# The first batch of an attention and feed-forward kernel, reordered as a pipeline: exponentials in a row, padding behind the first copies, second batch's scores and loads earlier, tail scores in one tile

## Chip, cores, metric

One core of a Trainium2 chip. The metric is the device time of one execution in microseconds (us), lower is better. Most executions of one kernel agree within a few tenths of a per cent, but some spread more (six of the changed kernel in e5: 431.95 to 436.08); all runs told here are of the fast state. A profile is one execution recorded by the hardware profiler; its span is the time from the first to the last instruction, some 1.8 us shorter than the time of the same execution.

## The reference

Attention with a relative position bias, then a bilinear feed-forward layer.

```python
B, H, S, D = 8, 8, 576, 64           # q, k, v: (8, 8, 576, 64), float32
scores = (q @ k^T) / 8 + bias[bucket(|i - j|)]          # bias per head
attn   = softmax(scores)
x      = (attn @ v), heads side by side                 # (4608, 512)
out    = ((x @ w_a) * (x @ w_b)) @ w_out                # d_ff = 1536
```

## The kernel before

The program is ordered by hand: each engine executes its instructions in the order in which the program gives them. Two heads are a "pair" `p`; there are 32 pairs, 4 for each of the 8 batches. A sequence of 576 is 512 main positions and 64 tail positions. The bias is applied after the exponential, as a multiplication by a stored band of exponentiated bias (`W_sb`, `Wt_sb`).

The first batch (pairs 0 to 3) runs by itself, in halves of 256 queries, because nothing else can run yet. From pair 4 on there is a "stage" `s` for each pair: scores and exponentials of pair `s`, outputs of pair `s-1`, and between them "units" of the feed-forward layer. A unit is four matmuls of 128x512 (0.86 to 0.88 us of TensorE), or of 128x256 for the first chunk's split part (0.44 us). `quotas` says how many units a stage gets; from stage 9 on it is 9.

```python
def padding():                       # constants: zeros and ones around the loaded values
    for i in range(2):
        nc.vector.memset(vt[i][0:64, :, 1, :], 0.0)
        ...                          # 12 memsets in all
# ... warm-up matmuls, bias table ...
nc.vector.tensor_copy(out=tab_sb[0:H, c0:c0 + NR], in_=tps[0:H, 0:NR])
padding()                            # VectorE: before any copy of q or k
# ... loads of q, k, v, weights, in the order of the diff below ...

def t_qk(p):                         # transpose q, k of a pair on TensorE, copy out of PSUM
    t_q(p, ACT if p == 0 else None)  # None: VectorE
    t_k(p, None, ps_ff)
def scores0(p, h):                   # scores of half h, then two exponentials on ScalarE
    qk_half(p, h); ex_half(p, h, 0); ex_half(p, h, 1)
def scale0(p, h):                    # two multiplications by the bias band on VectorE
    mul_half(p, h, 0); mul_half(p, h, 1)
    if h == 1: mul_tail(p)

def t_x(p, jqs=range(5), eng=None):  # transpose the outputs of a pair for the feed-forward layer
    if 4 <= p < NP - 1:
        ...                          # by two DMA transposes, issued by SyncE
        return
    ...                              # pairs 0 to 3 and 31: on TensorE, copied by eng

for c in range(NCH):                 # 9 chunks of 512 tokens
    if c == 0:
        parts = [(range(0, 6), 0, 256), (range(0, 6), 256, 256), (range(6, NDF), 0, 512)]
    else:
        parts = [(range(NDF), 0, 512)]
    ...                              # units of x@w_a, x@w_b, then 12 units of @w_out
```

`warm_up(n)` puts `n` dummy matmuls on TensorE. `av(p, jqs)` computes attention outputs and normalizes them on VectorE.

The softmax here doesn't subtract the row's maximum and nothing guards it: scores larger than these inputs give would overflow.

## Time and profile before

| | before |
|---|---|
| time, median of 3 | 436.48 us (435.53 to 437.32) |
| span of the profile | 434.5 us |
| TensorE busy | 410.5 us (94%) |
| first scores of the second batch (stage 4) | 41.37 us |
| stage 5, stage 8, stage 9 begin | 52.36, 81.84, 91.31 us |

The page of the kernel before shows busy tenths in 40 slices of the span (10.9 us each), and the clock granted to TensorE in tenths:

```profile
PE   6768799999999999999999999999999999999995
DVE  5577667656664666466745664566546651321320
ACT  3767667566665676566666665676566633223321
PEclk8999999999999999999999999999999999999999
```

TensorE (PE) is full from the sixth slice. Only the first 55 us hold idle time that could be won; after that every microsecond is one of matmuls. VectorE (DVE) and ScalarE (ACT) are not full anywhere, so in the first slices no engine is the limit: they wait for one another.

The order in time of ScalarE before, at the start (start, duration, engine, line, operation, output and input; in brackets the idle time before it and what ended it):

```profile
5.30 0.60 ACT L277 ACTIVATE QT_105<-trb 128x512 bf16<-128x512 bf16 x1 [2.12 <-PE trb L287]
8.54 1.02 ACT L378 ACTIVATE ath_0_0_273<-qkh_0_0_263 128x1024 bf16<-128x1024 f32 x1 [2.65 <-PE qkh_0_0_263 L372]
...
13.31 1.02 ACT L378 ACTIVATE ath_0_0_352<-qkh_0_0_342 128x1024 bf16<-128x1024 f32 x1
...
15.13 1.03 ACT L378 ACTIVATE ath_0_0_368<-qkh_0_0_358 128x1024 bf16<-128x1024 f32 x1
...
17.92 1.02 ACT L395 ACTIVATE att_113<-qkt_384 128x1024 bf16<-128x1024 f32 x1 [0.84 <-PE qkt_384 L393]
```

The `ath` rows are the exponentials of pairs 0, 2 and 3; the last is that of the tail keys, which ends the first half of the batch. A row takes 1.02 us but the next can start 0.92 us later. From 17.92 us, 23.45 us pass until stage 4, with 8 more exponentials and 4 tails in them (about 11 us of work at the pitch of these rows).

VectorE before, the end of the padding and the first copy:

```profile
4.56 0.28 DVE L182 MEMSET vt_103<- 64x260 bf16 x1
...
7.15 0.11 DVE L188 MEMSET XG_121<- 64x64 uint32 x1
7.29 0.42 DVE L279 COPY KT_109<-trk_234 128x512 bf16<-128x512 bf16 x1
```

The transposed k of pair 0 was ready at 5.6 us (its transposes start at 5.20 and take 0.41) and waited for the padding.

The stretches view for stages 4 to 8 of the kernel before: length, busy time of each engine, in parentheses instructions, then granted clock, DMA share, GB/s:

```profile
core 0: us, PE busy (x) PEld busy (x) DVE busy (x) ACT busy (x) POOL busy (x), PEclk, DMA share, GB/s
41.37:52.36 10.99, 9.32 (x109) 6.65 (x110) 6.52 (x16) 7.23 (x15) 2.97 (x4) 1.00 1.28 204
52.36:63.08 10.72, 9.90 (x108) 5.74 (x109) 7.17 (x19) 7.32 (x13) 9.79 (x14) 1.00 1.54 128
63.08:72.74 9.66, 9.51 (x99) 4.92 (x101) 7.13 (x17) 7.13 (x11) 8.18 (x13) 1.00 1.90 174
72.74:81.84 9.10, 8.93 (x86) 4.54 (x86) 6.18 (x16) 5.74 (x9) 5.33 (x8) 1.00 1.75 116
81.84:91.31 9.47, 8.57 (x83) 4.50 (x85) 4.83 (x13) 6.05 (x9) 4.49 (x7) 1.00 1.03 171
```

Stages 4 and 5 leave TensorE some room (9.32 of 10.99, 9.90 of 10.72), stages 6 and 7 almost none.

### The profile page before, as it was taken

Reading aid. Unit: us, or ns where it says so; the run is one execution under the profiler, and the core shown is the slowest. Engines: PE = TensorE matmul, PEld = TensorE weight load, DVE = VectorE, ACT = ScalarE, POOL = GpSimd, SP = SyncE. Lnnn points to the kernel's source line nnn. Section 1 sums busy time; section 2 is a strip of 40 time slices with the busy share of each in tenths; the row PEclk is TensorE's granted clock in tenths of the full one; section 3 lists DMA queues with packets and bytes.
Section 4 is the critical chain, followed back from the end, with each engine's and each line's share of the span. In section 5 each row is a group of like instructions: output and inputs, shape, how many; then the busy total and the mean of one; then the engine's idle time right before and its main releaser. Section 6 shows DMA issues by size and latency. Waiting matters only on the chain.

```text
span 434.5 us, 8785 instructions
## 1 busy us (share of the span) xinstructions
PE 410.5 (94%) x3426; PEld 210.0 (48%) x3477; DVE 238.9 (55%) x582; ACT 250.2 (58%) x362; POOL 130.0 (30%) x187
## 2 busy tenths in 40 slices
PE   6768799999999999999999999999999999999995
PEld 3446555445445544445455545454555454444442
DVE  5577667656664666466745664566546651321320
ACT  3767667566665676566666665676566633223321
POOL 9654398295009600780059004300000000000000
PEclk8999999999999999999999999999999999999999
DMA  9999999999339943998279907960420011002004
GB/s 124 203 209 189 202 119 175 142 142 157 55 63 142 157 78 63 116 157 103 48 104 161 128 16 112 140 87 16 88 84 6 15 39 74 0 9 89 0 2 97
DMA packets 139596, 42.46 MB, mean 98 GB/s; under 512 B 115962, under 2 KB 134938, under 8 KB 139554
## 3 DMA queue, kind: packets, MB, share of 16 engines
q0 software_dynamic: 81264, 18.89, 50.4%
q1 hardware_dynamic: 52850, 13.54, 20.6%
q10 hardware_dynamic: 5440, 9.47, 6.7%
q8 instruction: 27, 0.44, 0.4%
q14 instruction: 15, 0.12, 0.1%
HBM read 39.18 MB, written 9.45 MB: 112 GB/s over the span
## 4 chain that ended last, share of the span: by engine, by line
PE 86%; DVE 6%; ACT 4%; issue 2%; DMA 0%; ACTq 0%; DVEq 0%
DVE g_140 L520 1%; PE po_0_1422 L527 1%; PE po_0_2701 L527 1%; PE po_0_4581 L527 1%; PE po_0_3963 L527 1%; PE po_0_3332 L527 1%; PE po_0_2070 L527 1%; PE po_3_2846 L527 1%; PE po_3_4108 L527 1%; PE po_3_2215 L527 1%; PE po_3_3477 L527 1%; PE po_3_4726 L527 1%; PE po_3_5742 L527 1%; PE po_2_4698 L527 1%; PE po_2_3449 L527 1%
## 5 line engine op out<-in xcount | busy, mean ns | idle before, releaser
L158 POOL DMA_DIRECT2D vt_104<-in_v_dram x8 | 4.9, 619 | 62.4 <-PE av_3_2771 L467 27.6
L517 PEld LDWEIGHTS <-wb_126 128*128 128x128 bf16 x152 | 14.5, 97 | 18.6 <-issue 4.2
L507 PEld LDWEIGHTS <-wa_122 128*128 128x128 bf16 x160 | 15.1, 98 | 17.2 <-issue 1.8
L517 PEld LDWEIGHTS <-wb_125 128*128 128x128 bf16 x160 | 14.0, 97 | 18.1 <-issue 8.0
L507 PEld LDWEIGHTS <-wa_124 128*128 128x128 bf16 x144 | 13.3, 98 | 18.3 <-issue 3.4
L158 POOL DMA_DIRECT2D vt_103<-in_v_dram x8 | 5.0, 650 | 53.8 <-PE av_3_3402 L467 27.1
L507 PEld LDWEIGHTS <-wa_123 128*128 128x128 bf16 x152 | 13.2, 98 | 15.3 <-issue 3.6
L129 POOL DMA_DIRECT2D qn_93<-in_q_dram x24 | 18.4, 815 | 7.2 <-DMA wo<-in_moe_w_out_dram 5.9
L517 PEld LDWEIGHTS <-wb_127 128*128 128x128 bf16 x144 | 12.4, 97 | 16.6 <-issue 6.3
L138 POOL DMA_DIRECT2D kn_95<-in_k_dram x24 | 18.1, 800 | 3.7 <-PE av_2_847 L467 1.9
L129 POOL DMA_DIRECT2D qn_94<-in_q_dram x24 | 18.1, 802 | 1.1 <-DMA vt_103<-in_v_dram 0.6
L138 POOL DMA_DIRECT2D kn_96<-in_k_dram x24 | 18.1, 790 | 0.3 <-PE pb_9_0_1283 L517 0.3
L527 PEld LDWEIGHTS <-g_137 128*128 128x128 bf16 x36 | 3.5, 97 | 8.7 <-issue 6.8
L520 DVE TENSOR_TENSOR g_133<-pb_0_0_5542,ha_0_0_5540 128x512 bf16<-128x512 f32 x1 | 0.7, 692 | 11.4 <-PE pb_0_0_5542 L517 11.4
L205 PE MATMUL warm<-zero_sb 128*128 128x512 bf16 x13 | 5.6, 535 | 1.4 <-DVE zero_sb L197 1.2
L120 POOL DMA_DIRECT2D vn_97<-in_v_dram x8 | 6.3, 784 | 1.5 <-DVE rc_0_1185 L476 0.7
L120 POOL DMA_DIRECT2D vn_98<-in_v_dram x8 | 6.3, 784 | 1.1 <-DVE g_135 L520 0.8
L349 PEld LDWEIGHTS <-KB_116 64*128 64x128 bf16 x96 | 2.9, 94 | 7.5 <-issue 6.4
L527 PEld LDWEIGHTS <-g_133 128*128 128x128 bf16 x36 | 3.5, 98 | 4.6 <-issue 0.8
L527 PEld LDWEIGHTS <-g_139 128*128 128x128 bf16 x36 | 3.5, 98 | 4.3
L527 PEld LDWEIGHTS <-g_140 128*128 128x128 bf16 x36 | 3.5, 98 | 4.2
L527 PEld LDWEIGHTS <-g_135 128*128 128x128 bf16 x36 | 3.5, 98 | 4.3
(2939 smaller groups left out, 1524.7 us busy)
## 6 DMA issues: line engine op xcount, KB each, us to landing
vn_97<-in_v_dram POOLq DMA_DIRECT2D x8, 256.0 KB, 5.9
vn_98<-in_v_dram POOLq DMA_DIRECT2D x8, 256.0 KB, 6.6
wo<-in_moe_w_out_dram POOLq DMA_DIRECT2D x1, 1536.0 KB, 16.4
kn_95<-in_k_dram POOLq DMA_DIRECT2D x24, 64.0 KB, 5.4
qn_93<-in_q_dram POOLq DMA_DIRECT2D x24, 64.0 KB, 4.8
kn_96<-in_k_dram POOLq DMA_DIRECT2D x24, 64.0 KB, 4.6
qn_94<-in_q_dram POOLq DMA_DIRECT2D x24, 64.0 KB, 4.6
qn_93<-in_q_dram POOLq DMA_DIRECT2D x4, 128.0 KB, 4.2
```

The lines of the kernel that those rows point to most:

```text
L120: nc.gpsimd.dma_start(out=dst[:, 256 * h0:256 * h1].rearrange("p (h x) -> p h x", x=256), in_=src[b, h0:h1, 0:SM, :].rearrange("h (p t) d ...
L129: nc.gpsimd.dma_start(out=by_tile(qn[b % 2])[:, h0 // 4, t, :, :], in_=q[b, h0:h1, 128 * t:128 * t + 128, :].transpose([1, 0, 2]))
L138: nc.gpsimd.dma_start(out=by_tile(kn[b % 2])[:, h0 // 4, t, :, :], in_=k[b, h0:h1, t:SM:NM, :].transpose([1, 0, 2]))
L158: nc.gpsimd.dma_start(out=vt[b % 2][64 * hh:64 * hh + 64, :, hh, 0:Dh], in_=v[b, hh:H:2, SM:S, :].transpose([1, 0, 2]))
L205: nc.tensor.matmul(out=warm[:, :], lhsT=zero_sb[:, 0:128], rhs=zero_sb[:, :], start=True, stop=True)
L349: nc.tensor.matmul(out=ps[:, hh, :], lhsT=kT[r, t, :], rhs=qT[r, :, :], start=True, stop=True)
L507: nc.tensor.matmul(out=pa[:, 0:n], lhsT=wa_sb[df // 4][:, mc, 128 * (df % 4):128 * (df % 4) + 128], rhs=xn_sb[mc][:, 512 * c + lo:512 * c ...
L517: nc.tensor.matmul(out=pb[:, 0:n], lhsT=wb_sb[df // 4][:, mc, 128 * (df % 4):128 * (df % 4) + 128], rhs=xn_sb[mc][:, 512 * c + lo:512 * c ...
L520: nc.vector.tensor_tensor(out=g_sb[df][:, lo:lo + n], in0=pb[:, 0:n], in1=ff["ha"][:, 0:n], op=MULT)
L527: nc.tensor.matmul(out=po[:, :], lhsT=g_sb[df][:, 128 * tt:128 * tt + 128], rhs=wo_sb[:, df, :], start=(df == 0), stop=(df == NDF - 1))
```

## The change

The intent: let the exponentials of the first batch follow one another without gaps, so that the second batch's scores start earlier. The padding moves from in front of the first copies to behind the copies of pair 1; seven of the eight copies of attention outputs (`t_x`) go from ScalarE to VectorE; the tail scores of a first-batch pair share one PSUM tile and take one exponential and two multiplications instead of two and three (the later pairs keep two exponentials, but also take two multiplications instead of three); the loads of the second batch's q and k move ahead of weights. The feed-forward units are cut anew: the first chunk is split for four weight tiles instead of six (44 units instead of 48), only 4 of them stand before stage 4 instead of 8, and stages 6 and 7 get 7 instead of 6.

```diff
-    padding()                                   # (was in front of the first copies)
-            parts = [(range(0, 6), 0, 256), (range(0, 6), 256, 256), (range(6, NDF), 0, 512)]
+            parts = [(range(0, 4), 0, 256), (range(0, 4), 256, 256), (range(4, NDF), 0, 512)]
...                                              # tail: scores of tail x tail into the main tail tile
+        pt = ps[:, 1, n:n + ST] if n < SM else tr_half().bitcast(FP32)[:, 0:ST]
...
+    t_qk(0); warm_up(1); scores0(0, 0); t_qk(1)
+    padding()
+    load_rest()             # loads: q, k of batch 1 before parts 1 and 2 of the weights, w_out last
+    warm_up(1); scores0(1, 0); t_qk(2); scale0(0, 0)
+    warm_up(2); scores0(2, 0); t_qk(3); load_w_rest(); scale0(1, 0)
+    warm_up(2); scores0(3, 0); t_tails0(); scale0(2, 0); tail_keys0(); v_in(0, 0, 4)
+    sc(0, 0); sc(0, 1); av(0, h0); scale0(3, 0); tail0(0); av(1, h0, ps_ff, "ffn"); sc(1, 0)
...                          # sc: one tile of scores and its exponential; 4 units in all
-    quotas = {4: 12, 5: 8, 6: 6, 7: 6, 8: 6}
+    quotas = {4: 12, 5: 8, 6: 7, 7: 7, 8: 6}
...                          # stage 4: t_x(2), t_x(3) on VectorE, av(3) later
```

(The new lines of the order are put on fewer lines here; three dots mark cuts.)

More of the change, by code (lines that the diff above doesn't have):

```diff
@@ L99 @@
     KT = [wpool.tile([128, NM, 128], BF16, name=f"KT{i}") for i in range(4)]
-    att0 = wpool.tile([128, 4, 256], BF16, name="att0")
+    att = [wpool.tile([128, 1024 + 128], BF16, name=f"att{i}") for i in range(2)]
+    atk = wpool.tile([128, 4, 256], BF16, name="atk")
     QB = [wpool.tile([128, 2, NM, 2, 128], BF16, name=f"QB{i}") for i in range(2)]
@@ L188, in padding @@
             nc.vector.memset(XG[i][64:128, 4, :, :], 0.0)
+            nc.vector.memset(att[i][:, 512 + SM // 2 + ST:], 0.0)
     nc.sync.dma_start(out=bt_sb[0:NB, :], in_=bias_table)
@@ L243 @@
         load_k(0, h, h + 2)
-    load_tails(0)
-    load_v(0, 0, 4)
-    load_vt(0)
-    load_v(0, 4, 8)
-    load_w_in(0)
-    load_q(1, 0, 2)
-    load_k(1, 0, 2)
-    load_tails(1)
-    load_w_in(1)
-    load_q(1, 2, 4)
-    load_k(1, 2, 4)
-    load_v(1, 0, 4)
-    load_vt(1)
-    load_w_in(2)
-    load_q(1, 4, 6)
-    load_k(1, 4, 6)
-    load_w_out()
-    load_q(1, 6, 8)
-    load_k(1, 6, 8)
-    load_v(1, 4, 8)
     st = [dict() for _ in range(NP)]
@@ L362, in mul, with qk_half @@
                                 in1=w[:, :, S - 1 + t:S - 1 + t - SM:-1], op=MULT)
-    def qk_half(p, h):
+    def qk_half(p, h, us=(0, 1)):
         qT, kT, _ = operands(p)
-        for u in range(2):
+        for u in us:
             ps = ps_sc.tile([128, 2, 512], FP32, tag="sc", name=f"qkh{p}_{h}_{u}")
@@ L394, in tail_keys0 @@
                              rhs=qT[:, 0:2, :], start=True, stop=True)
-        nc.scalar.activation(out=att0[:, :, :].rearrange("p (a b) c -> p a (b c)", a=2),
+        nc.scalar.activation(out=atk[:, :, :].rearrange("p (a b) c -> p a (b c)", a=2),
                              in_=ps[:, :, :], func=ACTF.Exp, scale=scale)
@@ L405, in qk_tail @@
                 lhsT=kT[:, t, :], rhs=z[:, 0, :], start=True, stop=True)
-        q0 = 2 if p < 4 else 0
-        nc.tensor.matmul(out=ps[:, 1, 0:SM - 128 * q0], lhsT=z[:, 1, :], rhs=qT[:, q0:, :],
+        n = main_tail(p)
+        nc.tensor.matmul(out=ps[:, 1, 0:n], lhsT=z[:, 1, :], rhs=qT[:, (SM - n) // 128:, :],
                          start=True, stop=True)
-        pt = tr_half().bitcast(FP32)[:, 0:ST]
+        pt = ps[:, 1, n:n + ST] if n < SM else tr_half().bitcast(FP32)[:, 0:ST]
         for hh in range(2):
@@ L413, in qk_tail, with main_tail @@
         st[p]["ps"] = (ps, pt)
+    def main_tail(p):
+        return SM // 2 if p < 4 else SM
     def ex_tail(p):
-        hp = p % 4
         ps, pt = st[p]["ps"]
-        at = wrk.tile([128, ST + 1024], BF16, tag="att", name=f"att{p}")
-        nc.scalar.activation(out=at[:, 0:ST], in_=pt, func=ACTF.Exp, scale=scale)
-        n = 768 if p < 4 else 1024
-        nc.scalar.activation(out=at[:, ST:ST + n],
-                             in_=ps[:, :, :].rearrange("p a x -> p (a x)")[:, 0:n],
+        n = main_tail(p)
+        at = att[p % 2]
+        m = 512 + n
+        if n < SM:
+            m += ST
+        else:
+            nc.scalar.activation(out=at[:, m:m + ST], in_=pt, func=ACTF.Exp, scale=scale)
+        nc.scalar.activation(out=at[:, 0:m], in_=ps[:, :, :].rearrange("p a x -> p (a x)")[:, 0:m],
                              func=ACTF.Exp, scale=scale)
@@ L426, in mul_tail @@
     def mul_tail(p):
-        hp = p % 4
-        at, w, wt = st[p]["att"], W_sb[hp], Wt_sb[:, hp, :]
-        nc.vector.tensor_tensor(out=at[:, 0:ST], in0=at[:, 0:ST], in1=wt[:, ST - 1::-1], op=MULT)
-        x = at[:, ST:ST + 512].rearrange("p (h t c) -> p h t c", h=2, t=NM)
+        at, w, wt = st[p]["att"], W_sb[p % 4], Wt_sb[:, p % 4, :]
+        x = at[:, 0:512].rearrange("p (h t c) -> p h t c", h=2, t=NM)
         rev = w[:, :, ST - 1::-1]
@@ L434, in mul_tail @@
         nc.vector.tensor_tensor(out=x, in0=x, in1=e, op=MULT)
-        o = ST + 512 + (128 if p < 4 else 384)
-        nc.vector.tensor_tensor(out=at[:, o:o + 128], in0=at[:, o:o + 128],
-                                in1=wt[:, 191:63:-1], op=MULT)
+        o = 512 + main_tail(p) - 128
+        nc.vector.tensor_tensor(out=at[:, o:o + 192], in0=at[:, o:o + 192], in1=wt[:, 191::-1], op=MULT)
     def weights(p, t, hh, jq):
         if jq == 4:
-            o = ST + 256 * hh + ST * t
+            o = 256 * hh + ST * t
             return st[p]["att"][:, o:o + 128]
@@ L449, in weights_tail @@
         if jq == 4:
-            return st[p]["att"][:, 0:128]
+            o = 512 + main_tail(p)
+            return st[p]["att"][:, o:o + 128]
         if p < 4 and jq < 2:
-            return att0[:, p, 128 * jq:128 * jq + 128]
-        o = ST + 512 + 128 * (jq if p >= 4 else jq - 2)
+            return atk[:, p, 128 * jq:128 * jq + 128]
+        o = 512 + 128 * (jq if p >= 4 else jq - 2)
         return st[p]["att"][:, o:o + 128]
@@ L592, in tail0, with load_rest @@
         ex_tail(p)
+    def load_rest():
+        load_tails(0)
+        load_v(0, 0, 4)
+        load_vt(0)
+        load_v(0, 4, 8)
+        load_w_in(0)
+        load_q(1, 0, 2)
+        load_k(1, 0, 2)
+        load_tails(1)
+        load_q(1, 2, 4)
+        load_k(1, 2, 4)
+        load_w_in(1)
+        load_v(1, 0, 4)
+        load_vt(1)
+        load_q(1, 4, 6)
+        load_k(1, 4, 6)
+        load_w_in(2)
+        load_q(1, 6, 8)
+        load_k(1, 6, 8)
+        load_v(1, 4, 8)
+        load_w_out()
@@ L594 @@
     t_qk(0)
+    warm_up(1)
+    scores0(0, 0)
     t_qk(1)
-    scores0(0, 0)
+    padding()
+    load_rest()
+    warm_up(1)
+    scores0(1, 0)
+    t_qk(2)
+    scale0(0, 0)
     warm_up(2)
-    t_qk(2)
-    scores0(1, 0)
-    warm_up(2)
+    scores0(2, 0)
     t_qk(3)
     load_w_rest()
-    scale0(0, 0)
-    scores0(2, 0)
+    scale0(1, 0)
     warm_up(2)
     scores0(3, 0)
-    scale0(1, 0)
     t_tails0()
+    scale0(2, 0)
     tail_keys0()
     v_in(0, 0, 4)
-    scores0(0, 1)
-    warm_up(2)
@@ L613, with sc @@
-    av(0, (0, 1))
-    scale0(2, 0)
-    av(1, (0, 1), ps_ff, "ffn")
-    t_x(0, (0, 1), ACT)
-    v_in(0, 4, 8)
+    h0 = (0, 1)
+    h1 = (2, 3, 4)
+    def sc(p, u):
+        qk_half(p, 1, (u,))
+        ex_half(p, 1, u)
+    sc(0, 0)
+    sc(0, 1)
+    av(0, h0)
     scale0(3, 0)
     tail0(0)
-    av(2, (0, 1))
-    t_x(1, (0, 1), ACT)
-    scores0(1, 1)
-    av(3, (0, 1), ps_ff, "ffn")
-    t_x(2, (0, 1), ACT)
-    scale0(0, 1)
-    t_x(3, (0, 1), ACT)
-    tail0(1)
-    av(0, (2, 3, 4))
@@ L629 @@
-    scale0(1, 1)
+    av(1, h0, ps_ff, "ffn")
+    sc(1, 0)
+    v_in(0, 4, 8)
+    mul_half(0, 1, 0)
+    mul_half(0, 1, 1)
+    t_x(0, h0)
+    sc(1, 1)
+    av(2, h0)
+    mul_tail(0)
+    tail0(1)
+    t_x(1, h0)
+    av(3, h0, ps_ff, "ffn")
+    sc(2, 0)
+    mul_half(1, 1, 0)
+    av(0, h1)
+    mul_half(1, 1, 1)
+    t_x(2, h0)
+    sc(2, 1)
+    mul_tail(1)
+    tail0(2)
+    t_x(3, h0)
     t_tails(1)
-    qk_half(2, 1)
-    ex_half(2, 1, 0)
+    mul_half(2, 1, 0)
+    sc(3, 0)
+    t_x(0, h1, ACT)
@@ L634 @@
+    av(1, h1)
     put_units(1)
-    ex_half(2, 1, 1)
-    av(1, (2, 3, 4))
-    t_x(0, (2, 3, 4), ACT)
+    mul_half(2, 1, 1)
+    sc(3, 1)
+    t_q(4)
+    mul_tail(2)
     put_units(1)
-    tail0(2)
-    put_units(1)
-    scale0(2, 1)
-    t_x(1, (2, 3, 4), ACT)
-    qk_half(3, 1)
-    ex_half(3, 1, 0)
-    put_units(1)
-    ex_half(3, 1, 1)
-    av(2, (2, 3, 4))
-    put_units(1)
-    t_q(4)
     tail0(3)
-    put_units(1)
     t_k(4, ACT)
-    scale0(3, 1)
-    t_x(2, (2, 3, 4), ACT)
+    mul_half(3, 1, 0)
@@ L655 @@
+    av(2, h1)
+    t_x(1, h1)
     put_units(2)
+    mul_half(3, 1, 1)
+    mul_tail(3)
     load_half(2, 0)
     load_half(2, 1)
-    quotas = {4: 12, 5: 8, 6: 6, 7: 6, 8: 6}
+    quotas = {4: 12, 5: 8, 6: 7, 7: 7, 8: 6}
     for s in range(4, NP + 1):
@@ L667 @@
         if s == 4:
-            steps += [U, A(2, 3, 4), lambda: ex(s, 1), U, lambda: mul(s, 0), lambda: t_q(s + 1), U,
-                      lambda: mul(s, 1), lambda: t_x(s - 1, (2, 3, 4), ACT),
-                      lambda: (qk(s, 2), ex(s, 2)), U,
-                      lambda: ex(s, 3), lambda: t_k(s + 1, ACT), U,
+            steps += [U, lambda: ex(s, 1), lambda: t_x(2, h1), lambda: mul(s, 0), U, lambda: av(3, h1),
+                      lambda: t_q(s + 1), U, lambda: mul(s, 1), lambda: (qk(s, 2), ex(s, 2)),
+                      lambda: t_x(3, h1), U, lambda: ex(s, 3), lambda: t_k(s + 1, ACT), U,
                       lambda: mul(s, 2), U, lambda: mul(s, 3), U,
```

## The prediction

> **What bounds it now.** The stretches view gives TensorE 99% busy from 100 us on (19.64 of 20.00 us, 59.27 of 60.00). A row of twelve 512-wide matmuls takes 2.59 us, 216 ns each, which is the warm start-to-start that the Trainium skill gives ("TensorE: Matmul & The Clock Gate", "Wait — 56ns, not 53.3ns?"). So after the start the kernel is fixed TensorE work, and only the first ~60 us can give anything. There the chain of waits hops between all three engines. The first batch runs from 4.7 us to 41.37 us, where the first scores of the second batch (stage 4) issue. Its TensorE work, summed from the rows' pitches, is about 20 us of those 36.7. ScalarE has about 24.5 us of work there, in pieces with gaps of 1 to 2 us (an attention output copy waits for TensorE, the next exponential waits behind it). Stage 4 (41.37 to 52.5) and stage 5 (52.5 to 63.15) hold about 8.5 and 9.0 us of TensorE work, so some 2.6 and 1.7 us of slack. Stages 6 and 7 are nearly full.
>
> **What changes, costed.**
> - Padding (2.7 us of memsets, 4.56 to 7.29) stood before the first KT copy. Now that copy runs at about 5.7, and the first exponential starts near 6.5 instead of 8.54. But the padding then delays the copies of pair 2 to about 11.2, so ScalarE idles about 2 us there; the exponentials of tail keys start near 17 (17.92). Only about 1 us of the first 2 survives.
> - From there exponentials follow every 0.92 us. Seven of eight attention copies leave ScalarE in the first batch (0.38 or 0.50 us each) for VectorE.
> - Tail exponential in one: the two starts are 0.12 us apart, so 0.1 us saved for each of 4 tails; the merged multiplication saves about 0.1 us each.
> - VectorE becomes the limit of the first batch: about 27.5 us of work up to stage 4, nearly without gaps from 18 us. Walking the new order with the measured pitches (0.60 us a multiplication, 0.55 or 0.95 an output) puts the first stage-4 scores at 34 to 35.5.
> - Only 4 feed-forward units instead of 8 come before stage 4: 4 x 0.44 = 1.8 us given back. Stage 5 gets 8 full units instead of 4 half and 4 full: the same work, put into its slack. Units per chunk fall from 48 to 44 with the same matmul columns.
> - Loads: the same bytes, second-batch q and k ahead of weights, output weights last. I expect no new wait: weights part 1 land near 36 (needed about 45), part 2 near 46 (needed about 55). The rest of the bias bands land at 20.7 to 27.4 now and about 0.6 later afterwards, while needed from 21.8: one VectorE wait of up to 1 us.
>
> **Sum.** 6.5 us at stage 4, minus 1.8, plus 1 to 1.5 in stage 4, plus 1 in stages 5 to 7: about 7 us. All of it stays, since TensorE is full afterwards.
>
> Predicted 429.5 us, range 427.0 to 432.8; faster by over 2% 0.17, within 2% 0.82, slower 0.01.
>
> **What would show it.** First exponential near 6.5; first second-batch scores near 35 (41.37 now); stage 5 near 45.5 (52.5); stage 8 near 75 (81.84) with 38 of 44 units done; beyond 110 us the same 45.3 us per batch; VectorE over 90% busy from 20 to 36.
>
> **What would make it wrong.** Bias bands landing later than 28 (stalls VectorE, up to 2 us lost); the DMA order making the second batch's values or third batch's loads late; chunk boundaries now fall at the first unit of a stage, so a late transposed output of the last pair would stall TensorE once per batch; or in-order TensorE blocked behind VectorE more often than I walked through.

## The result

The change is 0.9% faster. Ratios here and below are the mean time of one kernel's fast runs over that of the kernel before in the same rounds, so they are not quite the ratio of the medians.

| | before | after |
|---|---|---|
| time, median of 4 | 436.31 us (435.53 to 437.32) | 432.19 us (432.11 to 432.51) |
| ratio, 95% interval | | 0.9906 (0.9884 to 0.9927) |
| span of the profile | 434.5 us | 430.5 us |
| first exponential | 8.54 us | 7.08 us |
| exponential of the tail keys | 17.92 us | 19.16 us |
| stage 4 begins | 41.37 us | 37.26 us |
| stage 5, 8, 9 begin | 52.36, 81.84, 91.31 | 48.21, 80.17, 89.33 |

The same lines of the page after:

```profile
PE   8689899999999999999999999999999999999995
DVE  5789667566654665466646664666546642321320
ACT  4676676676656666676566665676566642323221
PEclk9789999999999999999999999999999999999999
```

TensorE is busier in the first slices (in part because its matmuls took longer there, see the clock below), VectorE is 80% full or more in the third and fourth (21 to 43 us). The clock row now dips in the second and third slices, where before it dipped a little in the first.

ScalarE after, the exponentials that answer to those shown of before:

```profile
7.08 1.02 ACT L359 ACTIVATE ath_0_0_214<-qkh_0_0_204 128x1024 bf16<-128x1024 f32 x1 [1.11 <-PE qkh_0_0_204 L353]
...
13.67 1.02 ACT L359 ACTIVATE ath_0_0_330<-qkh_0_0_320 128x1024 bf16<-128x1024 f32 x1 [1.85 <-PE qkh_0_0_320 L353]
...
16.60 1.02 ACT L359 ACTIVATE ath_0_0_374<-qkh_0_0_364 128x1024 bf16<-128x1024 f32 x1 [0.99 <-PE qkh_0_0_364 L353]
...
19.16 1.02 ACT L376 ACTIVATE atk<-qkt_390 128x1024 bf16<-128x1024 f32 x1 [0.63 <-PE qkt_390 L374]
```

The first exponential is 1.5 us earlier than before, that of pair 2 already 0.4 us later, that of pair 3 1.5 us later, and the tail keys' 1.2 us later. The opening was to gain 1 us and lost 1.2.

VectorE after: the second copy, the padding, and the copy of pair 2's k behind it:

```profile
8.76 0.41 DVE L260 COPY KT_110<-trk_227 128x512 bf16<-128x512 bf16 x1
9.17 0.28 DVE L183 MEMSET vt_103<- 64x260 bf16 x1
...
12.12 0.19 DVE L190 MEMSET att_114<- 128x160 uint32 x1
12.23 0.63 DVE L260 COPY QT_107<-trb 128x512 bf16<-128x512 bf16 x1
12.77 0.41 DVE L260 COPY KT_111<-trk_306 128x512 bf16<-128x512 bf16 x1
```

The padding takes 3.06 us (9.17 to 12.23) and stands exactly between two pairs. TensorE has pair 2's transposes done by 10.8 us and can only wait. In the stretches view after, one microsecond at a time:

```profile
11.00:12.00 1.00, 0.35 (x2) 0.00 (x0) 0.57 (x6) 0.82 (x1) 0.00 (x0) 1.00 1.46 219
12.00:13.00 1.00, 0.00 (x0) 0.00 (x0) 0.92 (x4) 0.00 (x0) 0.94 (x2) 1.00 1.52 235
13.00:14.00 1.00, 0.76 (x10) 0.34 (x10) 1.00 (x3) 0.33 (x1) 1.00 (x2) 0.75 1.57 200
14.00:15.00 1.00, 1.00 (x18) 0.83 (x18) 0.72 (x2) 1.00 (x2) 1.00 (x3) 0.50 1.62 175
```

The third number from the right is the granted clock. After the idle stretch it falls to half, from 13.5 to 16.9 us, and again from 20.3 to 23.7 us. The Trainium skill ("TensorE: Matmul & The Clock Gate", "What's actually happening") says that the array runs at half clock unless it has been busy in a free-running window of about 3.4 us; the two dips here last 3.4 us each, which agrees.

The view writes a clock of 1.00 for all the time before 13 us, but TensorE's rows show half speed there too. Eight transposes of one shape take 0.64 us up to about 10 us, and 0.41 us from then on:

```profile
7.40 0.64 PE L268 MATMUL trb<-ident,qn_93 128*64 128x128 bf16 x8
...
10.17 0.41 PE L268 MATMUL trb<-ident,qn_93 128*64 128x128 bf16 x8
```

In the profile before they take 0.41 us already at 5.20 us, and a half-clock stretch follows from 8.4 to 11.9 us. So the two openings were not seen at the same clock, and the 1.2 us lost at the tail keys are not the padding's alone. The section on e4 puts the profiles side by side.

The stages after, in the same view as before:

```profile
core 0: us, PE busy (x) PEld busy (x) DVE busy (x) ACT busy (x) POOL busy (x), PEclk, DMA share, GB/s
37.26:48.21 10.95, 9.71 (x112) 6.98 (x113) 8.34 (x25) 6.79 (x13) 5.36 (x7) 1.00 1.44 190
48.21:60.03 11.82, 11.43 (x107) 5.74 (x109) 7.91 (x18) 7.95 (x13) 5.38 (x8) 1.00 1.63 181
60.03:70.55 10.52, 10.38 (x103) 5.32 (x104) 7.75 (x17) 7.29 (x11) 9.85 (x15) 1.00 1.90 161
70.55:80.17 9.62, 9.42 (x89) 4.98 (x90) 5.79 (x14) 6.12 (x9) 8.29 (x13) 1.00 1.80 149
80.17:89.33 9.16, 8.84 (x84) 4.50 (x86) 4.66 (x12) 6.21 (x9) 4.95 (x8) 1.00 1.66 172
```

Stage 4 is as long as before (10.95 against 10.99). Stages 5 to 7 took 31.96 us against 29.48, 2.48 more, for work worth four full units more (about 3.5 us), so they gained 1.0.

### The profile page after: what moved, and what is told of

Read it like the earlier page. It is cut to its first block, busy times and chain, and to the rows that moved or that the text cites. A ratio compares the mean times of both kernels' runs of the same rounds, so it can differ in the third digit from the quotient of the medians.

```text
span 430.5 us, 8709 instructions
## 1 busy us (share of the span) xinstructions
PE 412.0 (96%) x3406; PEld 210.3 (49%) x3459; DVE 238.0 (55%) x560; ACT 248.1 (58%) x346; POOL 130.0 (30%) x187
## 3 DMA queue, kind: packets, MB, share of 16 engines
q10 hardware_dynamic: 5440, 9.47, 7.1%
## 4 chain that ended last, share of the span: by engine, by line
PE 88%; DVE 7%; issue 2%; ACT 1%; DVEq 0%; ACTq 0%
PE warm L207 1%; DVE g_143 L505 1%; PE trb L268 1%; DVE att_113 L419 1%; PE po_2_4609 L512 1%; PE po_2_3999 L512 1%; PE po_2_3376 L512 1%; PE po_2_2753 L512 1%; PE po_2_2130 L512 1%; PE po_1_2670 L512 1%; PE po_1_3916 L512 1%; PE po_3_5650 L512 1%; PE po_0_5379 L512 1%; PE po_0_5084 L512 1%; PE po_0_3878 L512 1%
## 5 line engine op out<-in xcount | busy, mean ns | idle before, releaser
L492 PEld LDWEIGHTS <-wa_124 128*128 128x128 bf16 x160 | 14.7, 98 | 17.8 <-issue 3.9
L502 PEld LDWEIGHTS <-wb_128 128*128 128x128 bf16 x144 | 13.3, 97 | 20.3 <-issue 7.1
L159 POOL DMA_DIRECT2D vt_104<-in_v_dram x8 | 4.9, 626 | 58.9 <-PE av_3_2722 L452 27.7
L159 POOL DMA_DIRECT2D vt_103<-in_v_dram x8 | 5.1, 645 | 55.5 <-PE av_3_3345 L452 27.4
L139 POOL DMA_DIRECT2D kn_96<-in_k_dram x24 | 18.1, 795 | 0.2 <-PE pb_11_0_1307 L502 0.2
L419 DVE TENSOR_TENSOR att_113<-att_113,W_88 128x512 bf16<-128x512 bf16 x8 | 3.4, 426 | 14.2 <-ACT att_113 L409 14.2
L408 ACT ACTIVATE att_114<-trb 128x64 bf16<-128x64 f32 x14 | 3.1, 224 | 10.8 <-PE trb L392 10.8
L408 ACT ACTIVATE att_113<-trb 128x64 bf16<-128x64 f32 x14 | 3.1, 224 | 10.7 <-PE trb L392 10.7
L419 DVE TENSOR_TENSOR att_114<-att_114,W_91 128x512 bf16<-128x512 bf16 x8 | 3.4, 427 | 7.6 <-ACT att_114 L409 7.6
L121 POOL DMA_DIRECT2D vn_97<-in_v_dram x8 | 6.6, 828 | 0.0
```

Of the source, the lines that this page charges most:

```text
L121: nc.gpsimd.dma_start(out=dst[:, 256 * h0:256 * h1].rearrange("p (h x) -> p h x", x=256), in_=src[b, h0:h1, 0:SM, :].rearrange("h (p t) d ...
L139: nc.gpsimd.dma_start(out=by_tile(kn[b % 2])[:, h0 // 4, t, :, :], in_=k[b, h0:h1, t:SM:NM, :].transpose([1, 0, 2]))
L159: nc.gpsimd.dma_start(out=vt[b % 2][64 * hh:64 * hh + 64, :, hh, 0:Dh], in_=v[b, hh:H:2, SM:S, :].transpose([1, 0, 2]))
L408: nc.scalar.activation(out=at[:, m:m + ST], in_=pt, func=ACTF.Exp, scale=scale)
L419: nc.vector.tensor_tensor(out=x, in0=x, in1=e, op=MULT)
L492: nc.tensor.matmul(out=pa[:, 0:n], lhsT=wa_sb[df // 4][:, mc, 128 * (df % 4):128 * (df % 4) + 128], rhs=xn_sb[mc][:, 512 * c + lo:512 * c ...
```

## The experiments

Two questions: why stage 4 began at 37.26 and not near 35, and what happened to the gains afterwards. The theories for the opening are the padding (its 3.06 us stand on the chain between pair 1 and pair 2) and the clock (TensorE ran at half speed in two stretches). Twelve kernels ran, five rounds each beside the kernel before; all were correct, e1 to e4 on one chip and e5 to e12 on another. Where a run's expectation names a time of the changed kernel, it is the 432.2 us of the first measurement; on the other chip the same kernel measured 433.0, and the kernel before 437.7 in the same rounds, so across chips the ratios are to be compared and not the medians.

| run | stage 4 | stage 5 | stage 8 | stage 9 | third score tile of stage 9 | span | median us | ratio (95%) |
|---|---|---|---|---|---|---|---|---|
| before | 41.37 | 52.36 | 81.84 | 91.31 | 96.90 | 434.5 | 436.31 | 1 |
| after | 37.26 | 48.21 | 80.17 | 89.33 | 94.35 | 430.5 | 432.19 | 0.9906 (0.9884, 0.9927) |
| e1 padding in gaps | 34.84 | 45.80 | 77.68 | 86.85 | 93.02 | 429.2 | 432.25 | 0.9895 (0.9865, 0.9926) |
| e2 padding first | 36.06 | 47.01 | 78.89 | 88.06 | 93.09 | 429.3 | 431.57 | 0.9875 (0.9847, 0.9902) |
| e3 more warm-ups | 35.75 | 46.71 | 79.01 | 88.18 | 94.03 | 430.2 | 431.82 | 0.9891 (0.9856, 0.9927) |
| e4 e1 and e3 | 35.54 | 46.49 | 78.37 | 87.53 | 93.53 | 429.6 | 431.38 | 0.9869 (0.9842, 0.9897) |
| e5 after again | 37.87 | 48.82 | 80.92 | 90.08 | 96.72 | 432.9 | 433.01 | 0.9903 (0.9865, 0.9941) |
| e6 e1, stage 8 shorter | 35.13 | 46.09 | 77.97 | 85.42 | 91.66 | 429.2 | 431.32 | 0.9860 (0.9832, 0.9889) |
| e7 old units | 37.21 | 47.53 | 76.60 | 85.55 | 90.58 | 430.9 | 431.52 | 0.9866 (0.9838, 0.9894) |
| e8 old load order | 37.75 | 48.70 | 80.58 | 89.75 | 94.79 | 430.9 | 432.59 | 0.9883 (0.9853, 0.9913) |
| e9 e1 and e7 | 34.92 | 45.24 | 73.94 | 83.15 | 88.17 | 428.6 | 430.73 | 0.9848 (0.9817, 0.9878) |
| e10 e1, pair 7 on TensorE | 36.92 | 47.87 | 79.81 | 89.86 | 94.89 | 430.4 | 430.71 | 0.9848 (0.9819, 0.9877) |
| e11 e9, stages 5 to 7 filled | 35.50 | 45.82 | 76.82 | 86.29 | 91.88 | 429.4 | 431.78 | 0.9873 (0.9843, 0.9902) |
| e12 one copy earlier in stage 4 | 36.09 | 47.21 | 79.15 | 88.32 | 94.98 | 431.1 | 433.07 | 0.9901 (0.9870, 0.9931) |

Times at stages are of one profile each (us from the start of the span). They compare only between kernels with the same units: e6, e7, e9 and e11 have done other numbers of units by stage 8. The intervals are 0.5 to 0.8% wide, so most differences of 1 to 2 us between two of these kernels are not settled by times alone; the profile has to carry them. The gains asked about here are hardly larger than the scatter.

### e1: the padding taken apart

```diff
     nc.vector.tensor_copy(out=tab_sb[0:H, c0:c0 + NR], in_=tps[0:H, 0:NR])
+    pad_vt(0)                     # 4 memsets, VectorE idle here for 1.41 us
...
     scores0(0, 0)
+    pad_rest()                    # 6 small memsets
     t_qk(1)
-    padding()
...
     v_in(0, 0, 4)
+    pad_vt(1)                     # 4 memsets; the loads behind it are issued after it
```

> The changed kernel with its padding taken apart: first value-tail tile's memsets before the first KT copy, the small memsets after it, the second tile's after the first value copy, where VectorE idled (gaps of 1.41, 1.77 and 1.83 us). Padding theory (the 3.06 us of memsets between the pair-1 and pair-2 copies held the opening): exponential of pair 2 starts at 11 to 11.5 instead of 13.67, tail-key exponential at 17 or earlier instead of 19.16, second batch's first scores 1.5 to 2.2 us earlier than 37.26, time 1.5 to 2.2 us under the changed kernel's 432.2, so near 430.3. Clock theory (TensorE at half its clock at 13 to 16.5 and 20 to 23.6 us held it): under 0.7 us.

Measured: exponentials of pairs 1 and 2 run together from 9.42 us, so pair 2's first at about 11.3; the tail keys' at 16.86; stage 4 at 34.84, 2.4 us earlier than after; the clock was full from about 7 us on and did not fall again. The opening behaves as the padding theory says. The time did not follow: 432.25 us where 430.3 was expected. The 2.4 us of lead are still there at stage 9 (86.85 against 89.33) and shrink to 1.3 at its third scores (93.02 against 94.35). TensorE's rows of e1 in between:

```profile
86.85 0.82 PE L332 MATMUL qk<-QB,KB 64*128 64x512 bf16 x4
87.60 0.82 PE L494 MATMUL pa<-xn,wa 128*128 128x512 bf16 x3
89.41 0.38 PE L494 MATMUL pa<-xn,wa 128*128 128x512 bf16 x1 [0.99 <-DMA xn<-XG]
...
93.02 0.60 PE L332 MATMUL qk<-QB,KB 64*128 64x512 bf16 x4
```

The first unit of the second chunk waits in its fourth matmul for the transposed output of pair 7, the last pair of the second batch. Its DMA transpose was issued at 83.09 us and landed 6.3 us later.

### e2: the padding where it was

```diff
     nc.vector.tensor_copy(out=tab_sb[0:H, c0:c0 + NR], in_=tps[0:H, 0:NR])
+    padding()
...
     t_qk(1)
-    padding()
```

> The changed kernel with the whole padding put back in front of the first KT copy, nothing else. Padding theory: first exponential near 8.5 to 9, but pair 2 no later than now (13.67) and rather at 12.5, so 0 to 1 us better than the changed kernel: its place behind the first copies would then be worth nothing or a loss. If the move was worth what its intent says, this run is 1.5 to 2 us slower (434).

Measured: first exponential 8.46 (1.4 us later than after), pair 2's at 13.33, tail keys' at 17.98, stage 4 at 36.06: 1.2 us earlier than after. With everything else of the change, the old place of the padding is no worse in time (431.57, ratio 0.9875; the intervals overlap). The 1.5 to 2 us that the move was meant to bring are not there. That the old place is better is not shown: 36.06 at stage 4 equals the earliest of the changed start's five profiles (36.09, e12; see e4).

### e3: more warm-ups

```diff
-    warm_up(2)
+    warm_up(8)
     scores0(2, 0)
...
+    warm_up(2)
     tail_keys0()
+    warm_up(2)
...
     sc(0, 0)
+    warm_up(3)
     sc(0, 1)
```

> The changed kernel with 13 more dummy matmuls where TensorE only waits (6 before pair 2's scores, 4 around the tail keys, 3 between the two score tiles after them), padding where the change has it. Clock theory: granted clock stays at 1.0 from 11 to 30 us, the first outputs' matmuls take 0.065 us a pair instead of 0.11, first scores of the second batch 1 to 1.5 us earlier, time near 431. Padding theory: at most 0.5 us.

Measured: the clock was full from about 7 us on, pair 2's exponential came at 13.48 as after (the padding still holds it), pair 3's at 15.62 (16.60), the tail keys' at 18.05 (19.16), stage 4 at 35.75, 1.5 us earlier. These are the clock theory's numbers, in one profile. The later e12 is a check: it has the changed start without the added dummy matmuls, and in its profile the clock happened to be full from 6 to 19 us. Its exponentials of pair 3 (15.55) and of the tail keys (17.98) come when e3's do. So a full clock is worth about 1.1 us at the tail keys, however it comes about. The time, 431.82, is a gain of 0.4 us against the first measurement and is not clear of noise; at the second chunk it waited 0.7 us, as e1 did.

### e4: both

```diff
-    padding()                     # taken apart as in e1
-    warm_up(2)
+    warm_up(8)                    # and the other three warm-ups of e3
```

> Both edits together. If padding and clock are two separate losses: sum of e1's and e3's gains, 2.5 to 3.5 us under the changed kernel (429 to 429.7). If they are one loss (the idle stretch left by the padding is what lets the clock fall): no more than the larger of the two.

Measured: full clock from about 4 us, stage 4 at 35.54, no better than e1 alone (34.84); the dummy matmuls now stand in the way. So in these single profiles mending either one gains 1.5 to 2.4 us at stage 4, and mending both adds nothing: in e1's profile the clock had not fallen anyway. That the padding's idle stretch is what lets the clock fall is not shown; it also fell in three later profiles with e1's start.

How large each part is can't be said sharply, because the half-clock time at the start differs between executions of one program. This is every profile with the changed kernel's start, and every one with e1's ("slow until": when TensorE's rows first run at full speed; then the half-clock stretches that the view shows, each of 3.4 us or two or three times that; all in us):

| profile | start | slow until | half-clock stretches | stage 4 |
|---|---|---|---|---|
| after | changed | 10 | 13.5 to 16.9, 20.3 to 23.7 | 37.26 |
| e5 | changed | 17 | 20.7 to 24.1 | 37.87 |
| e7 | changed | 7.5 | 14.3 to 24.5 | 37.21 |
| e8 | changed | 10.5 | 13.9 to 17.3, 20.7 to 24.1 | 37.75 |
| e12 | changed | 6 | 19.1 to 22.6 | 36.09 |
| e1 | e1's | 7 | none | 34.84 |
| e6 | e1's | 10 | none | 35.13 |
| e9 | e1's | 5 | 18.6 to 22.0 | 34.92 |
| e10 | e1's | 9 | 29.6 to 33.1 | 36.92 |
| e11 | e1's | 10 | 16.9 to 23.7 | 35.50 |

The means are 37.2 and 35.5, so the mended padding gains 1.8 us on average. At like clock: e12 and e9 (9 and 8 us at half speed in all) differ by 1.2 us, after and e11 (17 us each) by 1.8 us. Within the changed start, e12 is 1.1 to 1.8 us before the four profiles with 17 to 21 us at half speed. So the padding and the clock each cost 1 to 2 us at stage 4, and part of e1's 2.4 us was its shorter time at half speed. These are estimates from one profile each; e10 does not fit them, and why was not looked into.

### e5: the changed kernel again

No edit: the same program, on another chip and beside other kernels.

> The changed kernel once more, unedited, so that the next three stand beside it on one chip: ratio to the kernel before 0.989 to 0.992, second batch's first scores at 37.3, and the half-clock stretches at the start again in its profile (if the profile shows none, they vary from run to run).

Measured: ratio 0.9903, stage 4 at 37.87; times from 431.95 to 436.08. Its start ran at half speed until about 17 us, where the first profile's did until 10: the transposes that take 0.41 us at 10.17 us above still take 0.64 here at 15.24.

```profile
15.24 0.64 PE L268 MATMUL trk<-ident,kn 128*64 128x128 bf16 x8
```

Its profile (434.63 us) also has what the first profile of the same program did not:

```profile
90.08 0.82 PE L330 MATMUL qk<-QB,KB 64*128 64x512 bf16 x4
90.83 0.82 PE L492 MATMUL pa<-xn,wa 128*128 128x512 bf16 x3
93.11 0.38 PE L492 MATMUL pa<-xn,wa 128*128 128x512 bf16 x1 [1.46 <-DMA kn<-in_k_dram]
```

The bracket names a load of k, but a matmul of these operands needs no k: the transposed output of pair 7 was issued at 86.33 and landed 6.7 us later, at 93.0, just before the matmul. (A wait for several semaphores is put down to the one that came last; here the DMA transpose fits.) In the first profile the same transpose was issued at 85.57 and landed after 4.6 us, at 90.2, for a matmul at 90.74: 0.6 us to spare. Before the change it landed at 90.7 (87.56 + 3.1) for a matmul at 95.96: 5.3 us to spare. So the change had used up the spare time, and whether the wait shows differs between executions. It occurs at the second chunk only; the list of TensorE's waits after 120 us has none of it.

Why the landing takes 3.1 us in one profile and 6.8 in another was not tested. The Trainium skill says that DMAs of all issuing engines run on the same 16 DMA engines ("DMA: Bandwidth & Descriptors", "Issuing engines are not separate DMA queues"); the share of those engines from 80 to 95 us (as the view counts it; it can exceed 1) was 1.15 in the profile before, 1.71 in the first one after, and 1.84 to 2.03 in those of e1, e2, e3, e5 and e12, where the landing took 5.0 to 6.8 us (3.1 and 4.6 in the other two). So the later landings are in heavier traffic. That fits, but no run changed the traffic alone.

### e6: two units moved in front of the second chunk

```diff
-    quotas = {4: 12, 5: 8, 6: 7, 7: 7, 8: 6}
+    quotas = {4: 12, 5: 8, 6: 7, 7: 7, 8: 4}          # on top of e1
```

> e1 (padding in the gaps) with 4 feed-forward units in stage 8 instead of 6, so two output units stand in front of the second chunk's first unit. In e1 the 2.4 us won at the start shrank to 1.3 in stage 9, where TensorE waited 1.0 us for the last pair's transposed output. If that wait is the reason: stage 9 takes 5.0 us to its third score tile again, the whole 2.4 us stays, end of the profile near 428.2 (e1 429.2), time about 1 us under e1. Rival (the loads have fallen behind and will make TensorE wait somewhere else): same end as e1.

Measured: the wait for the transposed output is gone, but with two units less in stage 8 TensorE runs into ScalarE: it waits 1.3 us at the start of stage 9, between the first two score tiles, for a tail exponential. From stage 9 to its third score tile it took 6.24 us, not the expected 5.0. Span 429.2, as e1. The rival's number, by another wait than it named. The median is 0.9 us under e1's, from another chip, and not clear.

### e7: the old units

```diff
-            parts = [(range(0, 4), 0, 256), (range(0, 4), 256, 256), (range(4, NDF), 0, 512)]
+            parts = [(range(0, 6), 0, 256), (range(0, 6), 256, 256), (range(6, NDF), 0, 512)]
-    quotas = {4: 12, 5: 8, 6: 7, 7: 7, 8: 6}
+    quotas = {4: 12, 5: 8, 6: 6, 7: 6, 8: 6}
```

> The changed kernel with the first chunk split as before (six pairs of halves, 48 units) and the old quotas 12, 8, 6, 6, 6. The prediction gave 1 us to filling the slack of stages 5 to 7, so this should lose 0.5 to 1 us: lead over the kernel before at stage 8 only 3.5 to 4 us with the same units done, end near 431.3. If only the total of matmul columns counts, no loss.

Measured: the opposite. Median 431.52 against the changed kernel's 433.01 in the same rounds (ratios 0.9866 and 0.9903; the intervals overlap). TensorE's rows of e7:

```profile
37.21 0.60 PE L330 MATMUL qk<-QT,KT 64*128 64x512 bf16 x4
...
47.53 0.81 PE L330 MATMUL qk<-QT,KT 64*128 64x512 bf16 x4
...
85.55 0.82 PE L330 MATMUL qk<-QB,KB 64*128 64x512 bf16 x4
...
90.58 0.61 PE L330 MATMUL qk<-QB,KB 64*128 64x512 bf16 x4
```

Stage 4 took 10.32 us instead of 10.95. With four split tiles the second halves begin after 8 units, four into stage 4, and need the outputs of pair 3 that VectorE has just made; with six they begin four units later. Six units of the first chunk stand in front of the second when stage 9 begins, and there is no wait for pair 7. Stages 5 to 7 do lose time against the changed kernel, as expected, and it is more than made up. From stage 10 to stage 31 e7 took 236.81 us (96.90 to 333.71) and the changed kernel 237.88 (100.82 to 338.70); why the later phase of the units saves 1.1 us there I did not find out.

### e8: the old load order

```diff
-        load_q(1, 2, 4); load_k(1, 2, 4); load_w_in(1); load_v(1, 0, 4); load_vt(1); ...; load_w_out()
+        load_w_in(1); load_q(1, 2, 4); load_k(1, 2, 4); load_v(1, 0, 4); load_vt(1); load_w_in(2); ...
```

> The changed kernel with the loads in the old order. The prediction expects no effect: every load arrives before its use in both orders, so within 0.3 us of the changed kernel. If moving the second batch's loads up was needed for the earlier stage 4, its transposes of q and k wait and stage 4 or 5 begins 1 us or more later.

Measured: 432.59 us against 433.01, stage 4 at 37.75 (37.87), stage 5 at 48.70 (48.82). No effect that can be seen, as predicted.

### e9: e1 and e7 together

```diff
-    padding()                                          # taken apart as in e1
-    quotas = {4: 12, 5: 8, 6: 7, 7: 7, 8: 6}           # and the split tiles range(0, 4)
+    quotas = {4: 12, 5: 8, 6: 6, 7: 6, 8: 6}           # as in e7, range(0, 6)
```

> e1's padding in the gaps and e7's old chunk split and quotas. If the two edits mend different losses (e1 the start, e7 the wait at the second chunk): second batch's first scores at 34.8 to 35.2, stage 4 in 10.3 us, no wait for a transposed output in stages 8 to 10, time 1 to 2 us under both e1 and e7, ratio near 0.982 (faster by nearly 2%). If the loss is conserved (any us won at the start waits later for a load): ratio 0.986 as e7.

Measured: stage 4 at 34.92 and in 10.32 us, no wait for a transposed output, median 430.73 (429.85 to 431.73), ratio 0.9848: 1.5% under the kernel before. It is 0.8 us under e7's median and 1.5 us under e1's (e7 from earlier, e1 from the other chip; the ratios are 0.9848, 0.9866 and 0.9895), within the expectation for one and not the other. The ratio lies between the two that were expected (0.982 if the edits add up, 0.986 if not), so it does not decide between them. All six of its runs are below all six of e5's, on the same chip. They were run at other times.

### e10: the last pair's outputs transposed on TensorE

```diff
-        if 4 <= p < NP - 1:
+        if 4 <= p < NP - 1 and p != 7:                  # on top of e1; pair 7 in two pieces
```

> e1 with the last pair of the second batch transposed on TensorE and copied by VectorE instead of by the DMA, all else as e1. If stage 9 in e1 lost its 1.2 us to that DMA transpose alone: stage 9 to its third scores 5.0 to 5.4 us, no TensorE wait over 0.3 us there, end near 428.2, ratio 0.985 to 0.987. If another wait takes its place (batch loads, ScalarE), the end stays at 429.2.

Measured: from stage 9 to its third scores 5.03 us (86.85 to 93.02, 6.17, in e1), ratio 0.9848. So the lost 1.2 us at e1's stage 9 were that DMA transpose. But stage 8 grew to 10.05 us from e1's 9.17, 0.4 of it a wait for a copy, so most of them were given back in this profile. The profile is the slowest of the six runs (432.22; the clock's dip at 29 to 33 us), so its span says nothing against the median.

### e11: stages 5 to 7 filled, with six split tiles

```diff
-    quotas = {4: 12, 5: 8, 6: 6, 7: 6, 8: 6}
+    quotas = {4: 12, 5: 11, 6: 7, 7: 6, 8: 6}           # on top of e9
```

> e9 with quotas 12, 11, 7, 6, 6, so that stages 5 to 7 are filled as the change fills them (46 of 48 units done at stage 9, two left in front of the second chunk). Filling theory (stages 5 to 7 have 1 us or more of slack): ends 1 to 2 us under e9. If TensorE work is conserved or the second chunk waits again: same as e9 or worse.

Measured: 431.78, no better than e9 (430.73). TensorE waited 1.2 us for ScalarE at stages 8 and 9. The filling gains nothing that lasts in this form.

### e12: one copy earlier in stage 4

```diff
-    U, lambda: mul(s, 1), lambda: (qk(s, 2), ex(s, 2)), lambda: t_x(3, h1), U,
+    U, lambda: t_x(3, h1), lambda: mul(s, 1), lambda: (qk(s, 2), ex(s, 2)), U,
```

> The changed kernel with one call moved in stage 4: the copy of the last first-batch output stands before the second multiplication on VectorE, not after it. Stage 4 took 10.95 us in the changed kernel and in e1 to e5 whatever came before, against 10.99 before the change, where the prediction gave it 1 to 1.5 us. If VectorE's order before the second halves of the first chunk is what holds it: stage 4 in 10.0 to 10.5 us. If TensorE or ScalarE hold it: 10.9 again.

Measured: stage 4 took 11.12 us, longer. The wait for that copy (0.5 us after) went, but TensorE, in order, now stood 0.8 us behind the copy of the next q before it could transpose. So VectorE's order alone is not the reason; that the second halves come so early is (e7, e9 and e11: 10.32 us each).

## Why the prediction was right, and where not

The measured 432.19 us lies inside the range of 427.0 to 432.8, near its upper end; the class (within 2%) was right. That it lies inside is partly the width of the range: the gain in the spans is 4.0 us where about 7 were predicted, and e5's median, 433.01, would lie outside (on a chip where the kernel before was 1.3 us slower too). Term by term, from the two first profiles:

| term of the sum | predicted | measured |
|---|---|---|
| stage 4 begins earlier | 6.5 | 4.1 (41.37 - 37.26) |
| four units fewer before it | -1.8 | -1.8 (4 x 0.44) |
| in stage 4 | 1 to 1.5 | 0.0 (10.99, 10.95) |
| in stages 5 to 7 | 1 | 1.0 |
| from stage 8 on | 0 | 0.7 (the rest; 0.3 of it stage 8, 9.47 to 9.16) |

- What bounds it. Right: TensorE full after the start, and what is won at the start mostly stays. Not fully: "All of it stays, since TensorE is full afterwards" is not true of e1, where half of 2.4 us went again at the second chunk.
- The first term was mis-sized, by 2.4 us. "Only about 1 us of the first 2 survives": none did, and the tail keys' exponential came 1.2 us later than before. The pipeline behind it was costed well: from that exponential to stage 4 took 18.1 us (19.16 to 37.26), and the prediction's walk gave about 17.8 (17 to 34.8, the middle of its range). The padding was seen to delay pair 2 and its 2.7 us taken from the trace of before; it took 3.06 with the two memsets that the change adds. What was missing was the clock: a half-clock stretch at 8.4 to 11.9 us stands in the profile before, and I gave it no cost. e12 splits the loss: with the same start and a fuller clock its tail keys come at 17.98, as before (17.92), so in these profiles the padding takes up the whole gain of the opening (before's own half-clock stretch included), and the half clock of the first profile adds the other 1.2 us. e1 and e3 mend the one or the other; e2 shows that the old place of the padding would have been no worse.
- The third term was wrong. The slack of stage 4 was taken for room; in fact the new split of the first chunk asks for the last outputs earlier. e7, e9 and e11 shorten the stage by 0.63 us with the old split; e12 shows it is not one badly placed copy.
- The fourth was right in size, but e7, e9 and e11 show that kernels without this filling end no later, so it isn't a gain of the change in the end. The prediction also contradicted itself here: its marker "stage 8 near 75" gives stages 5 to 7 the 29.5 us that they took before, as if the four added units (3.5 us) cost nothing, where its sum counts 1 us. Stage 8 began at 80.17, 5.2 us after the marker, of which stage 5 (48.21 against 45.5) explains 2.7.
- Tail exponentials in one, load order: predicted small and none. The load order was tested (e8); the tail alone was not.
- VectorE "over 90% busy from 20 to 36": 12.90 of 14.00 us from 22 to 36, but 13.13 of 16.00 from 20, because the opening was late.
- Bias bands: no VectorE wait for them was seen. The feared late transposed output did come, in e1, e3, e4, e5 and e12, though once and not "once per batch".

The best versions, e9 and e10, reach 430.7 us, 1.5% under the kernel before (ratio 0.9848 both); the changed kernel measured 433.01 on the same chip before (e5, ratio 0.9903). The intervals of e9 and of e5 overlap a little (0.9817 to 0.9878 and 0.9865 to 0.9941), so that they beat it is likely and not settled by the ratios alone.

## What to carry to other kernels

Constants that must be written some time belong in the gaps an engine already has, not in one block; look for such gaps in the trace on both sides of where the block would stand. When a start is shortened, recheck the spare time of every transfer that was comfortable before, since the first tight one takes part of the gain and may do so only in some executions. An idle stretch of TensorE at the start can cost twice, once as a wait and once as a half clock after it (1.9 us, then 3.4 us at half clock, in the first profile after); that the one brought the other was not tested apart. Before two starts are compared, check in TensorE's rows that both ran at the same clock; here one and the same start ran at half speed for 9 to 21 us, depending on the execution.

## What the Trainium skill lacked or had wrong

- "TensorE: Matmul & The Clock Gate", "HAM oscillation — how this bites in real kernels", gives the rule of no idle gaps over about 3.4 us. Here the clock fell to half after an idle stretch of 1.9 us (11.35 to 13.24 us in the profile after), and again at 20.3 us after three microseconds in which TensorE was busy 0.48, 0.70 and 0.45 of the time without any gap over 0.8 us. So the rule, read as a limit below which an idle gap is safe, does not hold here. (The page's next section tells of a kernel whose clock falls after frequent short idles; it gives no length or share at which that begins.) The profile after, from 17 us:

```profile
17.00:18.00 1.00, 0.48 (x8) 0.36 (x9) 0.42 (x1) 1.00 (x2) 1.00 (x3) 1.00 1.28 201
18.00:19.00 1.00, 0.70 (x8) 0.26 (x5) 0.75 (x2) 0.54 (x1) 0.50 (x2) 1.00 1.25 206
19.00:20.00 1.00, 0.45 (x6) 0.21 (x5) 1.00 (x3) 0.84 (x1) 0.60 (x1) 1.00 1.21 210
20.00:21.00 1.00, 0.76 (x8) 0.38 (x8) 0.22 (x1) 1.00 (x3) 0.00 (x0) 0.66 0.99 148
```

- No page that I read gives a spread for the landing of a DMA transpose next to ordinary loads: the same transpose landed after 3.1 us in the profile before and 4.6 to 6.8 us in those of the changed kernel and of e1, e3, e5 and e12.
